# One pool of PSUM banks, exps of one to three banks, plain loads of x, and a new order for a gated mix of two attentions

## The chip, the core and the metric

The kernel runs on one core of a Trainium2 chip. The metric is device time in microseconds, 673.3 before the change (median of two runs, 673.2 and 673.4). A core has five engines with a queue each, worked off in order: TensorE (PE, whose weight loads the profile lists apart as PEld), VectorE (DVE), ScalarE (ACT), GpSimd (POOL) and SyncE (SP), which here only issues DMAs. Engines wait for each other through semaphores. PE writes its results into PSUM, eight banks of 512 fp32 columns on 128 partitions; ACT and DVE read them there and write SBUF.

## The reference

Two attentions over the same x (2048 rows of 512, 32 heads of width 16) are mixed by a gate of each row. A is linear attention with a learned feature map, B is softmax attention:

```python
x = A_x
g = sigmoid((x * gate_w).sum(-1, keepdims=True))

# A: q, k, v = x @ A_wqkv, split into heads
phi = lambda t: concat([softmax(t @ w_phi), softmax(-(t @ w_phi))])   # per head
kv, z = phi(k).T @ v, phi(k).sum(rows)
a = (phi(q) @ kv) / (phi(q) @ z + 1e-6) @ A_wo

# B: q, k, v = x @ B_wqkv, split into heads
p = softmax(q @ k.T * 16 ** -0.5)                                     # 2048 x 2048 per head
b = (p @ v) @ B_wo

return g * a + (1 - g) * b
```

Nearly all of the time goes into B's 32 x 2048 x 2048 exponentials and the matmuls before and behind them.

## The kernel before

**Blocks and tiles.** B's attention is cut into 32 blocks. A block has four heads (one in each quarter of the partitions) and one chunk of 512 queries. Its scores are 64 tiles: for each of the 16 tiles of 128 keys and each of the four heads one matmul of 32 rows (16 of them real) that writes a whole bank with 128 keys by 512 queries (`qk_mm`, line 966). The four heads' matmuls use different rows of PE's array and can run side by side. In all there are 2048 such tiles.

**Two ways to an exponential.** A tile goes one of two ways. On ACT's way one activation (line 1057) reads two neighbouring banks and writes `exp` to the buffer `E`. On DVE's way a `tensor_scalar` (line 1043 for one bank, 1033 for a pair of banks in one instruction) adds a constant and writes the sum as int16, whose bits are a coarse exponential in bf16; POOL then adds fixed steps to the words (`int64_add`, line 1019) for a second and a third, shifted copy, and the three are summed by the matmuls that follow, which evens the error out. A group is four such tiles, with two buffers for its copies. The constant list `DN` says how many tiles of each block go to DVE, 744 in all in 195 groups; the other 1304 are ACT's, in 652 exps.

**Sums over keys.** The weighted sum of the values (and, by a column of ones, the softmax denominator) is made by matmuls of 32 columns each (`pv_mm`, line 1078), four heads side by side on different columns of the array: one such round for a tile of keys from ACT, three for a group from DVE. All rounds of a block add up in one bank, `psO`. When the block is complete, DVE copies the bank out (line 1172), the denominators go through memory by several DMAs on SP (`ld`, `lq`), are inverted (line 1181), spread by two more steps (`lr`, `rb`) and multiplied in (line 1188). The last two blocks are turned on DVE instead (lines 1198 to 1208).

**Banks.** Six banks `S0` to `S5`, one `M` and one `O`. The exps of ACT alternate between `S0, S1` and `S2, S3`, so the scores of an exp are written when the exp two places before has been read. `S4`, `S5` and `M` serve DVE's tiles and all projections; `O` is the sum's.

**Around it.** All projections (`fill`, with `columns` on line 727 or full-width matmuls), A's feature maps (two exps on ACT for each, line 1334), its sums and its quotient, and the output projections (`out_tile`, `out_part`, `out_last`) are put between the work of B's attention wherever a bank is free. For two output tiles, 14 and 15, the part that needs no result of the last blocks is made ahead into `osum` (line 1262) and the rest is added later (line 1232).

**x.** PE needs x transposed. The first 512 rows come by four plain loads (line 651), on SP and ACT, and are transposed on PE against an identity (line 1453), with copies by ACT and DVE (lines 1459 and 1462). The other 1536 rows come by twelve transposing DMAs on SP (line 655).

**The order.** `Plan` holds every operation with what it reads and writes. `TABLE` gives each engine's order as a list of operation numbers, and, in `homes`, the bank of each result; a planner had made it ahead of time, with costs and due times that stand among the constants. `place` follows the lists, makes each operation that takes a bank wait for the one that last read it, and `emit` writes out the instructions with their semaphore waits.

## Time and profile before

| | |
|---|---|
| median of two runs | 673.3 us |
| span of the profiled execution | 675.3 us |
| PE busy | 660.0 us, 8695 instructions |
| ACT busy | 642.5 us, 723 instructions |
| DVE busy | 605.0 us, 965 instructions |
| POOL busy | 404.9 us, 432 instructions |
| mean granted TensorE clock | 0.989 |
| DMA | 30.92 MB |

The page gives the profiled execution's span, from the first to the last instruction, 675.3 us; its own time is not given apart from that. Busy time of PE counts each matmul from its start to the end of its pipeline, and matmuls overlap, so a busy PE is not one at its peak. In a line of a group, the first number behind the bar is the time the engine was busy with the group, the second the mean of one instruction in ns, and then follows the idle time just before them, with what ended it. In a line of the order of time, the first number is the start, the second the length, and a bracket holds the idle time before it.

### The profile page before, as it was taken

What the parts mean: (1) busy time and instruction counts of PE and PEld (TensorE: products, weight loads), DVE (VectorE), ACT (ScalarE), POOL (GpSimd) and SP (SyncE); (2) the same over time, 40 slices, a digit from 0 to 9 for tenths busy, and PEclk for the clock granted to TensorE, in tenths of its full rate; (3) what the DMA queues carried; (4) which work ended last, traced back from release to release, by engine and by line L of the source; (5) the groups of instructions that cost most, each with busy time, mean ns of one, the idle gap of its engine ahead of it and who ended that gap; (6) DMA issues with size and microseconds to landing.
All of it is one profiled execution on the core that took longest, in us unless ns stands there. A gap on an engine that the chain in (4) does not pass through costs nothing.

```text
span 675.3 us, 20326 instructions
## 1 busy us (share of the span) xinstructions
PE 660.0 (98%) x8695; PEld 226.8 (34%) x8695; DVE 605.0 (90%) x965; ACT 642.5 (95%) x723; POOL 404.9 (60%) x432
## 2 busy tenths in 40 slices
PE   8999999999999999989999999999999999999997
PEld 4332333434233333323233233322333232332332
DVE  4698889999998889989989999899999989999994
ACT  5999999999999999989999999999989998899995
POOL 7055466556656445656576776656675567565853
PEclk8999999999999999989999999999999999899999
DMA  7810101001010000000103222141112522034131
GB/s 127 171 26 11 31 14 27 9 7 29 7 27 11 14 16 9 16 16 9 27 26 78 79 49 74 39 110 42 29 42 70 110 51 77 17 84 95 27 95 33
DMA packets 67466, 30.92 MB, mean 46 GB/s; under 512 B 52696, under 2 KB 62296, under 8 KB 67376
## 3 DMA queue, kind: packets, MB, share of 16 engines
q1 hardware_dynamic: 66368, 28.95, 19.3%
q8 instruction: 68, 1.11, 0.8%
q10 hardware_dynamic: 576, 0.52, 0.2%
q0 software_dynamic: 432, 0.15, 0.2%
q14 instruction: 22, 0.18, 0.1%
HBM read 7.87 MB, written 8.88 MB: 25 GB/s over the span
## 4 chain that ended last, share of the span: by engine, by line
PE 63%; ACT 24%; DVE 7%; DMA 3%; SPq 2%; issue 1%; ACTq 0%; DVEq 0%
PE psO L1078 24%; PE psS L966 22%; ACT E_t L1057 22%; PE psS L727 12%; PE psS L1341 2%; DVE Tx_t L1043 2%; ACT EA_t L1334 1%; PE psS L818 1%; DVE Ty_t L1043 1%; DMA xT_t<-in_A_x_dram 1%; PE psS L831 1%; ACT phiK_t L1334 1%; DMA Lq_t<-ld 1%; DVE Wp_t L1043 1%; PE psS L1381 1%
## 5 line engine op out<-in xcount | busy, mean ns | idle before, releaser
L1057 ACT ACTIVATE E_t<-psS 128x1024 bf16<-128x1024 f32 x652 | 612.3, 1079 | 21.6 <-PE psS L966 18.2
L966 PE MATMUL psS<-qz_t,kTB_t 32*128 32x512 bf16 x2048 | 279.8, 386 | 8.6 <-ACT E_t L1057 2.6
L1043 DVE TENSOR_SCALAR Tx_t<-psS 128x512 int16<-128x512 f32 x260 | 170.7, 680 | 11.8 <-PE psS L966 10.8
L966 PEld LDWEIGHTS psS<-qz_t,kTB_t 32*128 32x128 bf16 x2048 | 74.3, 91 | 245.3 <-ACT E_t L1057 98.0
L1078 PE MATMUL psO<-E_t,vaug_t 128*32 128x512 bf16 (+1 forms) x1304 | 107.5, 389 | 0.0
L1019 POOL INT64_ADD vA_t<-vA_t x72 | 73.0, 1017 | 31.4 <-PE psO L1078 24.1
L1043 DVE TENSOR_SCALAR Ty_t<-psS 128x512 int16<-128x512 f32 x114 | 76.3, 683 | 7.9 <-PE psS L966 7.1
L1019 POOL INT64_ADD Ty_t<-Tx_t x29 | 29.7, 1023 | 37.2 <-DVE Tx_t L1043 31.6
L1078 PE MATMUL psO<-vA_t,vaug_t 128*32 128x512 bf16 x520 | 50.8, 384 | 0.0
L1019 POOL INT64_ADD Ty_t<-Ty_t x42 | 43.6, 1038 | 11.2 <-PE psO L1078 11.1
L1043 DVE TENSOR_SCALAR Tz_t<-psS 128x512 int16<-128x512 f32 x66 | 44.4, 683 | 6.1 <-PE psS L966 5.7
L1043 DVE TENSOR_SCALAR oT_t<-psS 128x512 int16<-128x512 f32 x60 | 40.5, 684 | 4.6 <-PE psS L966 4.3
L1078 PE MATMUL psO<-Ty_t,vaug_t 128*32 128x512 bf16 x436 | 44.2, 387 | 0.0
L1078 PEld LDWEIGHTS psO<-E_t,vaug_t 128*32 128x32 bf16 (+1 forms) x1304 | 26.8, 96 | 39.4 <-issue 27.7
L1043 DVE TENSOR_SCALAR vA_t<-psS 128x512 int16<-128x512 f32 x56 | 37.7, 682 | 1.9 <-PE psS L966 1.5
L1043 DVE TENSOR_SCALAR Wp_t<-psS 128x512 int16<-128x512 f32 x52 | 35.0, 684 | 2.6 <-PE psS L966 2.1
L1043 DVE TENSOR_SCALAR WAT_t<-psS 128x512 int16<-128x512 f32 x54 | 36.2, 682 | 1.1 <-PE psS L966 0.4
L727 PE MATMUL psS<-xT_t,WB_t 128*32 128x512 bf16 x480 | 36.8, 393 | 0.0
L727 PE MATMUL psS<-Wp_t,xT_t 128*32 128x512 bf16 x512 | 36.2, 382 | 0.0
L1019 POOL INT64_ADD vA_t<-Tx_t x22 | 21.9, 999 | 19.4 <-DVE Tx_t L1043 14.0
L1019 POOL INT64_ADD oT_t<-oT_t x18 | 17.8, 990 | 23.8 <-PE psO L1078 23.8
L1019 POOL INT64_ADD phiQT_t<-Tx_t x19 | 18.4, 971 | 20.1 <-DVE Tx_t L1043 15.7
(159 smaller groups left out, 876.7 us busy)
## 6 DMA issues: line engine op xcount, KB each, us to landing
dpq<-EA_t SPq DMA_DIRECT2D x16, 256.0 KB, 2.4
...
```

Source lines behind the costliest of these rows:

```text
L727: ins = e.matmul(out[32 * i:32 * i + 32, :], lhsT=lhsT[:, 32 * i:32 * i + 32], rhs=rhs, start=start, stop=stop, tile_position=(0, 32 * i))
L818: mms = [lambda e, ap, i=i, t=t: e.matmul(ap[:, 128 * i:128 * (i + 1)], lhsT=xT[:, t, NQ * c + 128 * i:NQ * c + 128 * (i + 1)], rhs=W_B[:, ...
L831: mms = [lambda e, ap, i=i, t=t: e.matmul(ap[:, 256 * i:256 * (i + 1)], lhsT=xT[:, t, NQ * c + 128 * (2 * hf + i):NQ * c + 128 * (2 * hf + ...
L966: return e.matmul(bank, lhsT=kT_B[32 * i:32 * i + 32, ROW[b // 2] % 2, 128 * kt:128 * (kt + 1)], rhs=qz[32 * i:32 * i + 32, b // 2 % 4, b ...
L1019: op = P.add("pool", P64 + W64 * size, d_prio(g["ts"][0]) - 5.0 + (0.0 if key == "s" else M_LATE), lambda e: e.int64_add(words(dst), words ...
L1043: ops.append(drain(f, mm, "dve", 0.70, d_prio(d), lambda e, ap, q=q: e.tensor_scalar(quarter(tb, q).bitcast(I16), ap, EXPB, 0.0, op0=ALU.a ...
L1057: op = P.add("act", EXP_OVH + 0.4267 * n, 0.0, lambda e: e.activation(Ebuf[:, j // 2 % EPAIRS, 512 * SZ[0] * (j % 2):512 * SZ[0] * (j % 2) ...
L1078: return e.matmul(psO[32 * i:32 * i + w, :], lhsT=vaug[:, kt, o:o + w], rhs=rhs, start=start, stop=stop, tile_position=(0, 32 * i), skip_g ...
L1334: ins = e.activation(dst.rearrange("p (g s c) -> p s g c", s=2, c=64)[:, sgn, :, :], ap.rearrange("p (g c) -> p g c", c=64), ACTF.Exp, sca ...
L1341: mms = [lambda e, ap, n=n, f=f: e.matmul(ap[:, 64 * n:64 * n + 64].rearrange("p (s g j) -> p s g j", s=2, j=4), lhsT=ident[:], rhs=es[n][ ...
L1381: ins = e.matmul(ap[64 * s:64 * s + 64, 68 * gg:68 * gg + 68], lhsT=phiK[:, m, 128 * g + 64 * s:128 * g + 64 * s + 64], rhs=vA[:, m, s, g, ...
```

## The change

One tensor `ps` holds all eight banks, and scores, projections and sums take any of them: every single score tile is now an operation with a bank of its own (`tile_mm`), and each block's sum has its own `Fill` in the pool, so that two blocks' sums can be open at the same time. An exp reads one, two or three banks at equal distance, as the string `sizes` says (620 of two, 17 of three, 5 of one), and writes them side by side into a ring of 24 slots of `E`. `acts` lists the tiles of keys that ACT takes (four heads each, 324 of them, 1296 tiles), `groups` those that DVE takes (188 groups of four heads, 752 tiles) with the buffers of their copies. A sum's round is always the four heads of one tile of keys. Pairs of DVE's tiles in one instruction go from 41 to 71. The planner's constants (costs, priorities, due times) are gone from the kernel; the order of each engine's list, the banks and the pairs are new throughout.

x comes by seven plain loads, five on SP and two on ACT, and all 16 tiles are transposed on PE (line 1453 before, now in a loop over `NT`), 15 of the copies on DVE and one on ACT.

What each block and each projection computes is unchanged.

```diff
+ESLOTS = 24
+XLOADS = (("sp", 0, 1), ("act", 1, 2), ("sp", 2, 3), ("act", 3, 4), ("sp", 4, 8), ("sp", 8, 12), ("sp", 12, 16))
+XACT = (1,)
+WENG = ("sp", "pool", "sp", "sp", "sp", "sp")
...
-    psS = ctx.enter_context(nc.psum_tensor("psS", [128, 3584], F32))
-    psO = ctx.enter_context(nc.psum_tensor("psO", [128, 512], F32))
-    psM = psS[:, 3072:3584]
-    bS = [Bank(f"S{i}", psS[:, 512 * i:512 * (i + 1)], i) for i in range(6)]
-    bO = Bank("O", psO[:])
-    bM = Bank("M", psM, 6)
...
+    ps = ctx.enter_context(nc.psum_tensor("ps", [128, 4096], F32))
+    ps3 = ps[:].rearrange("p (a c) -> p a c", c=512)
+    banks = [Bank(f"S{i}", ps[:, 512 * i:512 * (i + 1)], i) for i in range(8)]
...
-    xs = phiK[:, 0:2, :].rearrange("p a b -> p (a b)").rearrange("p (i c) -> p i c", i=4)
-    for i in range(4):
-        dma("sp" if i % 2 == 0 else "act", -0.01, lambda e, i=i: e.dma_start(
-            xs[:, i, :], A_x[0, 128 * i:128 * (i + 1), :]), [("xs", i)], name=f"xs{i}", issue=0.45, lat=2.65 if i < 2 else 2.9)
-    for c in range(1, QC):
-        for t in range(KT):
-            dma("sp", 0.01 * (4 * c + t), lambda e, c=c, t=t: e.dma_start_transpose(
-                xT[:, t, NQ * c:NQ * (c + 1)], A_x[0, NQ * c:NQ * (c + 1), 128 * t:128 * (t + 1)]),
-                [("xT", t, c)], name=f"x{c}_{t}", issue=1.4, lat=3.9)
+    xs = phiK[:].rearrange("p a b -> p (a b)").rearrange("p (i c) -> p i c", c=D)
+    x_v = A_x[0].rearrange("(i p) c -> p i c", p=128)
+    for n, (eng, lo, hi) in enumerate(XLOADS):
+        dma(eng, lambda e, lo=lo, hi=hi: e.dma_start(xs[:, lo:hi, :], x_v[:, lo:hi, :]), [("xs", i) for i in range(lo, hi)],
+            name=f"xs{n}")
...
+    def tile_mm(b, i, kt, name, after=()):
+        f = Fill()
+        op = P.add("pe", lambda e: e.matmul(f.ap(), lhsT=kT_B[32 * i:32 * i + 32, ROW[b // 2] % 2, 128 * kt:128 * (kt + 1)],
+                                            rhs=qz[32 * i:32 * i + 32, b // 2 % 4, b % 2, :], start=True, stop=True,
+                                            tile_position=(32 * i, 0)),
+                   reads=[kkey(ROW[b // 2], kt), ("q", b // 2 % 4, b % 2)], after=after, name=name)
+        op.acq, op.att, op.shape = f, ("s", b, kt, i), ("row", i)
+        return f, op
...
+    def add_round(quad, parts, reads, name, after=()):
+        b, kt = divmod(quad, 16)
+
+        def fn(e):
+            for i in range(4):
+                ins = pv_mm(e, b, i, kt, parts(i), op.opens, op.closes)
+            return ins
...
-        op = P.add("act", EXP_OVH + 0.4267 * n, 0.0, lambda e: e.activation(
-            Ebuf[:, j // 2 % EPAIRS, 512 * SZ[0] * (j % 2):512 * SZ[0] * (j % 2) + 512 * n], psS[:, 512 * base:512 * (base + n)], ACTF.Exp, scale=ESCALE),
-            reads=[("S", j % 2)], writes=[("E", j % ERING)], name=f"exp{j}")
...
+        def fn(e):
+            where = sorted(f.bank.index for f, _ in slot)
+            step = where[1] - where[0] if n > 1 else 1
+            assert step > 0 and all(y - x == step for x, y in zip(where, where[1:]))
+            return e.activation(Ebuf[:, 512 * k:512 * (k + n)].rearrange("p (a c) -> p a c", c=512), ps3[:, where[0]:where[-1] + 1:step, :],
+                                ACTF.Exp, scale=ESCALE)
...
-            P.add("dve", 0.69, -50, lambda e: e.tensor_copy(Tf[:, par, :], psO[:]), reads=["psO"], writes=[("Tf", par)],
-                  after=[pv], name=f"ev.{b}").kind = "ev"
+            P.add("dve", lambda e: e.tensor_copy(Tf[:, par, :], psum(b)), writes=[("Tf", par)], after=pv, name=f"ev.{b}").fills = (P.sums[b],)
...
-    for i in range(4):
+    xe = []
+    for i in range(NT):
         mms = [lambda e, ap, i=i, t=t: e.transpose(ap.bitcast(BF16)[:, 128 * t:128 * (t + 1)],
                                                    xs[:, i, 128 * t:128 * (t + 1)], ident[:]) for t in range(KT)]
```

The beginning of the new lists of SP and PE, with the numbers written out as operations: SP issues x tile 2, the first keys' weights, x tile 0, x tiles 4 to 7, x tiles 8 to 11, the first values' weights, x tiles 12 to 15. PE transposes x tiles 1, 0, 2 and 3, makes the first queries and keys, transposes tiles 7 and 4, begins the first values, transposes tile 5, ends the first values, and then makes the first three score tiles.

994 lines of the change are left out of this document (374 added, 620 removed), and 519 rows, old and new, of the table TABLE.

## The prediction

> **What bounds the kernel now.** I read the page's busy shares first, then the same by stretches of time, then the groups, then the waits, and last the order of time in four places: start, a full stretch, two holes, the end.
>
> ```profile
> PE 660.0 (98%) x8695; PEld 226.8 (34%) x8695; DVE 605.0 (90%) x965; ACT 642.5 (95%) x723; POOL 404.9 (60%) x432
> ```
>
> ```profile
> 0.00:10.00 10.00, 8.30 (x61) 4.95 (x61) 6.60 (x26) 4.24 (x6) 8.91 (x18) 1.00 0.75 151
> 10.00:20.00 10.00, 8.73 (x78) 3.63 (x78) 1.55 (x3) 6.94 (x8) 4.51 (x9) 0.66 0.71 99
> 20.00:665.00 645.00, 636.00 (x8443) 215.44 (x8446) 592.70 (x929) 627.24 (x707) 390.28 (x405) 0.99 0.19 43
> 665.00:676.00 11.00, 6.95 (x122) 2.79 (x114) 4.14 (x7) 4.04 (x5) 1.17 (x2) 0.93 0.15 49
> ```
>
> The columns are the stretch, its length, then PE, PEld, DVE, ACT and POOL busy, the granted clock, and DMA. ACT stands still for 32.8 us of the 675.3: 5.8 before 10 us, 3.1 up to 20, 17.8 in the 645 us of the middle, 6.3 at the end (665 to 675.3). PE is busy almost throughout, but that row counts a matmul's pipeline, so the waits must say whether PE waits or makes others wait.
>
> ```profile
> PEld psS L966 <- ACT E_t L1057: 98.0, 239, 0.8
> PEld psO L1078 <- issue: 82.6, 330, 0.4
> ACT E_t L1057 <- PE psS L966: 18.2, 41, 1.5
> ```
>
> PE's weight load waits 239 times for an exp to give a bank back, 0.41 us each; where it waits for nothing the pause is 0.25 (82.6/330). So about 0.16 x 239 = 38 us are real waits of PE for ACT, against 18.2 us in 41 waits of ACT for PE. ACT bounds the middle, with PE a close second, and DVE (592.7 of 645) third. What ACT needs at least:
>
> ```profile
> L1057 ACT ACTIVATE E_t<-psS 128x1024 bf16<-128x1024 f32 x652 | 612.3, 1079 | 21.6 <-PE psS L966 18.2 <-PE psO L1078 2.3
> L1334 ACT ACTIVATE phiK_t<-psS 128x512 bf16<-128x512 f32 x32 | 18.3, 660 | 0.0
> 308.62 22.23 ACT L1057 ACTIVATE E_t<-psS 128x1024 bf16<-128x1024 f32 x24 [0.23 <-PE psS L966]
> ```
>
> One exp of two banks lasts 1.079 us, but 24 in a row take 22.23, which is (22.23 - 1.08)/23 = 0.92 from one to the next. All 652 at that pace are 600 us.
>
> **The change part by part.** Counts are from both kernels' written-out orders, each number matched to its operation by the order in which the builder makes them.
>
> *Exps.* 652 of two banks become 620 of two, 17 of three, 5 of one (the string of sizes); 1304 tiles become 1296. A three-bank or one-bank exp is not in the trace. The nearest rows are 1024 columns (1079) and 512 columns (660): a bank more or less is 0.42 us. So 620 x 0.92 + 17 x 1.34 + 5 x 0.50 = 595.7, **-4.1 us** on the engine that bounds. More is excluded, since no row shows a bank under 0.42. Bounds: -3.6 if a bank costs half of a two-bank exp (0.46), 0 if a read of three banks, which need not adjoin, takes 0.24 longer than that (4.1/17).
>
> *DVE's tiles.* 744 become 752, and pairs in one instruction 41 become 71.
>
> ```profile
> L1043 DVE TENSOR_SCALAR Ty_t<-psS 128x512 int16<-128x512 f32 x114 | 76.3, 683 | 7.9 <-PE psS L966 7.1
> L1033 DVE TENSOR_SCALAR Ty_t<-psS 128x1024 int16<-128x1024 f32 x7 | 8.5, 1218 | 0.0
> L1019 POOL INT64_ADD vA_t<-vA_t x72 | 73.0, 1017 | 31.4 <-PE psO L1078 24.1 <-DVE vA_t L1043 7.1
> ```
>
> Before 662 x 0.683 + 41 x 1.22 = 502 us, after 610 x 0.683 + 71 x 1.22 = 503: nothing. POOL's adds go from 390 to 376 at 1.02 us; POOL is 60% busy and the rest of its time hides any change; without that cover it would be -14 us.
>
> *PE in the middle.* Sums of a block come in whole rounds of four matmuls: 343 + 585 = 928 rounds before (ACT's tiles and three for each of 195 groups, some only half filled), 324 + 3 x 188 = 888 after. Scores come in bursts between them: 583 before, 643 after.
>
> ```profile
> 661.25 0.61 PE L727 MATMUL psS<-WoB_t,oT_t 128*32 128x512 bf16 x8
> 661.79 0.39 PE L966 MATMUL psS<-qz_t,kTB_t 32*128 32x512 bf16 x2
> 662.11 0.40 PE L727 MATMUL psS<-WoB_t,oT_t 128*32 128x512 bf16 x4
> 662.33 0.60 PE L727 MATMUL psS<-WoA_t,phiK_t 128*32 128x512 bf16 x8
> ```
>
> A round starts 0.22 after the last (662.11 to 662.33). Two rounds and the way into a burst take 0.54, so the way in costs 0.11; burst to round takes 0.32, so the way out costs 0.10. A burst thus costs 0.21 beside its matmuls. Rounds: -40 x 0.22 = -8.8. Bursts: +60 x 0.21 = +12.6. Matmuls that queue on the same rows of the array inside a burst: 724 become 715, -1.9. Together about **+2** of PE work. More matters where it falls. I went through both orders and added up PE's work between the last scores of one exp and of the next. Before, 219 of 581 such stretches are above ACT's 0.92, by 75 us in all, and the trace made 17.8 us of idle ACT of that. After, 276 of 600 are above it, by 93. In the same proportion ACT idles 22.1: **+4.3 us**. Bounds: 0 (PE's 38 us of waiting takes it), +18 (all of the growth is paid).
>
> Of the Trainium skill, "TensorEngine Tiling (Array Packing)", section Key Properties, speaks against this change: a change of tiling mode drains TensorE. The 0.11 and 0.10 agree with it in kind; by that rule alone each of the 60 bursts more would put 0.21 on the path, and the sum below would be 8 us higher.
>
> *One pool of banks.* Before, an exp's two banks are fixed and its scores wait for the exp two places earlier. In the new table, of the 581 exps that take a bank over from ACT, 559 still take it from two places earlier, 18 from three, 4 from the one before. So the pool deepens nothing for ACT. It does let a block's sum start in another bank while the last one is still being read, and the trace has one place where that hurts, and one where DVE waits for a reciprocal's way through memory:
>
> ```profile
> 570.00:580.00 10.00, 9.48 (x121) 3.11 (x113) 8.54 (x12) 7.19 (x9) 6.92 (x8) 0.83 0.06 16
> 576.42 1.89 PE L1078 MATMUL psO<-E_t,vaug_t 128*32 128x512 bf16 x14
> 577.50 1.94 ACT L1057 ACTIVATE E_t<-psS 128x1024 bf16<-128x1024 f32 x2 [2.34 <-PE psO L1078]
> 290.00:300.00 10.00, 8.49 (x78) 2.59 (x82) 7.87 (x12) 6.82 (x8) 3.67 (x4) 0.83 0.00 0
> 292.40 1.40 DVE L1188 TENSOR_TENSOR oT_t<-Tf_t,Rb_t 128x512 bf16<-128x512 f32 x1 [1.15 <-DMA Rb_t<-lr]
> ```
>
> These two stretches hold 2.8 + 3.2 = 6.0 us of idle ACT. They are accidents of this one order, so a new order does not inherit them: **-6.0**. Bounds: -6.0, and 0 if it has as many of its own (between reciprocal and product it leaves 13 to 20 DVE instructions, against 14 to 26).
>
> *Start.* x chunks 1 to 3 now come by three plain loads and go through 48 more transposes on PE and 12 more copies on DVE, in place of twelve transposing DMAs.
>
> ```profile
> 0.73 0.87 SPq L651 DMA_DIRECT2D phiK_t<-in_A_x_dram  x2
> 2.67 16.54 SPq L655 DMA_TRANSPOSE xT_t<-in_A_x_dram  x12
> 4.57 1.22 PE L1453 MATMUL psS<-ident_t,phiK_t 128*128 128x128 bf16 x12
> 4.82 0.42 DVE L1462 COPY xT_t<-psO 128x512 bf16<-128x512 bf16 x1 [0.69 <-PE psO L1453]
> 7.85 0.40 PE L966 MATMUL psS<-qz_t,kTB_t 32*128 32x512 bf16 x4
> 8.28 3.77 ACT L1057 ACTIVATE E_t<-psS 128x1024 bf16<-128x1024 f32 x4 [1.08 <-PE psS L966]
> 10.00:12.00 2.00, 0.73 (x10) 0.36 (x10) 0.00 (x0) 2.00 (x3) 2.00 (x6) 1.00 0.70 110
> 12.00:19.00 7.00, 7.00 (x57) 2.62 (x56) 1.39 (x2) 4.15 (x5) 1.97 (x4) 0.51 0.74 96
> WvA_t<-in_A_wqkv_dram SPq DMA_DIRECT2D x1, 512.0 KB, 4.3
> ```
>
> SP's queue loses 16.5 us of issues. PE gains 48 x 0.10 = 4.9 us and DVE 12 x 0.42 = 5.0, both where PE had a hole (10 to 12 us) and DVE 8.4 us free. What can be won is ACT's 3.1 us between 10 and 20, when x came late and the clock stood at 0.51. What can be lost: in the new PE order two transposes of chunk 1 and the first values' projection stand ahead of the first scores, and its weights are sixth on SP, behind two of the 512 KB loads. Such a load lands 4.3 us after its issue; two issues take 0.87, so the weights' turn comes near 0.7 + 5 x 0.44 = 2.9 us, and landing 4.3 to 8.6 later is 7.2 to 11.5, against first scores at 7.85 and a first exp at 8.28. So the first exp is 0 to 3.3 later (the projection's own 0.4 would lie on top). I take half of that, 1.6, and the whole gain: **-1.5**; bounds -3.1 and +3.3.
>
> *End.* After the last sum's turn DVE now has two partial outputs and two outputs; before, the first of these partials was done at 663:
>
> ```profile
> 662.56 0.75 DVE L1262 TENSOR_SCALAR xT_t<-psS,gT_t 128x512 f32<-128x512 f32 x1 [0.76 <-PE psS L727]
> 670.34 0.71 DVE L1262 TENSOR_SCALAR xT_t<-psS,gT_t 128x512 f32<-128x512 f32 x1
> 671.14 1.41 DVE L1232 SCALAR_TENSOR_TENSOR WB_t<-psS,gT_t,xT_t 128x512 bf16<-128x512 f32 x2
> ```
>
> One more at 0.71: **+0.7**. Blocks 30 and 31 are now halved between ACT and DVE (32 tiles of 64 each; 32 and 16 were DVE's); I count that at nothing, with up to 2 us won of the 6.3.
>
> *Sum.* 675.3 - 4.1 + 4.3 - 6.0 - 1.5 + 0.7 = 668.7. The timed runs (673.2 to 673.4) lie 2.0 below the profiled span, so **666.7, say 667 us**. With its bounds on the middle the case runs from 658 to 681.
>
> **The rivals.** *The holes close.* ACT's 17.8 idle us in the middle, and the 12 us by which its 612.3 busy us exceed 652 x 0.92, are the price of waiting at all. If the new order feeds ACT steadily, half of these 30 us go instead of 6.0 less 4.3: 667 - 13 = 654. For it: each score tile now has a bank, and a wait, of its own, and the bursts are more even (396 of three). Against it: the distance of two exps is as before, and more stretches are over 0.92.
>
> *PE becomes the bound.* The 60 bursts more and their unevenness are paid in full, 18 in place of 4.3, the two holes come back elsewhere (+6), and the start loses 1.6 instead of winning: 667 + 13.7 + 6.0 + 3.1 = 690. It decides from the point where PE's work between two exps is above 0.92 so often that its 38 us of waits no longer take it up. For it: 276 against 219 such stretches. Against it: total PE work grows by less than 1% of 660.
>
> *It does not do what it says.* The pool is mostly used as the fixed pairs were (559 of 581), tiles and work move by 1%. Then only -4.1 and the start count: 668, which is inside the forecast.
>
> **How the numbers follow.** Forecast 0.35, does not do what it says 0.10 (the same time, so 0.45 for the two), holes close 0.32, PE the bound 0.23. Fewer than 2% from no change is 659.8 to 686.8; about that much a measurement of this kernel can tell. Faster: nearly all of the second case and the low edge of the first, 0.33. Slower: most of the third, 0.19. Within: 0.48. The range goes from 651 (the second case less its start) to 691 (the third). The likeliest case's own range is 658 to 681.
>
> **What would show it.** Exps: the two-bank group at 620 or so and the pace still 0.92. PE: scores' waits for ACT well below 98 us and ACT's wait for scores above 18.2 if bursts cost what I say; the reverse if the holes close. Start: ACT's idle time between 10 and 20 us gone, the first exp near 9 to 10 us. Block changes: no idle ACT of over 2 us put down to the sums. The forecast is wrong if ACT's idle time from 20 us to the last 10 is under 10 us or above 35.

## The result, and the profile after

The changed kernel takes **696.9 us** (median of two runs, 696.4 and 697.4) against 673.3: a ratio of 1.036, with an interval of 1.031 to 1.042. It is slower, and outside the forecast's range (651 to 691). The profiled execution has a span of 694.6 us and was timed at 696.4, so a timed run lies 1.8 above its span; the forecast had set it 2.0 below. One thing is needed to read the times: executions of one and the same kernel differ by some 2% with the TensorE clock that they were granted, so each ratio below is made against runs of the kernel before on the same chip, with disturbed ones left out.

The busy shares and the stretches of the changed kernel, cut as the prediction cut them (stretch, length, PE, PEld, DVE, ACT, POOL busy, clock, DMA):

```profile
PE 673.4 (97%) x8759; PEld 231.6 (33%) x8759; DVE 627.4 (90%) x955; ACT 645.6 (93%) x713; POOL 408.2 (59%) x418
```

```profile
0.00:10.00 10.00, 6.71 (x37) 3.67 (x38) 4.36 (x22) 2.58 (x4) 8.46 (x17) 0.86 0.82 229
10.00:20.00 10.00, 9.50 (x103) 5.54 (x101) 8.35 (x21) 6.59 (x6) 0.00 (x0) 0.97 0.76 154
20.00:684.30 664.30, 650.76 (x8516) 219.94 (x8518) 609.91 (x906) 635.12 (x702) 397.06 (x399) 0.98 0.17 40
684.30:695.00 10.70, 6.45 (x116) 2.47 (x108) 4.81 (x8) 1.27 (x2) 2.64 (x3) 0.92 0.15 51
```

ACT now stands still for 7.4 us up to 10 (5.8 before), 3.4 up to 20 (3.1), 29.2 in the middle (17.8) and 9.0 at the end (6.3). Two waits, and the groups of exps by size with one run of exps in the order of time:

```profile
PEld ps L892 <- ACT E_t L975: 117.9, 303, 0.8
ACT E_t L975 <- PE ps L892: 29.2, 45, 3.9
```

```profile
L975 ACT ACTIVATE E_t<-ps 128x1024 bf16<-128x1024 f32 x620 | 588.2, 1035 | 28.3 <-PE ps L892 24.5 <-PE ps L903 0.8
L975 ACT ACTIVATE E_t<-ps 128x1536 bf16<-128x1536 f32 x17 | 24.7, 1459 | 5.0 <-PE ps L892 4.8
L975 ACT ACTIVATE E_t<-ps 128x512 bf16<-128x512 f32 x5 | 3.0, 606 | 0.0
```

```profile
353.04 18.53 ACT L975 ACTIVATE E_t<-ps 128x1024 bf16<-128x1024 f32 x20
```

A third bank costs 1459 - 1035 = 424 ns, and the pace of two-bank exps in a row is (18.53 - 1.03)/19 = 0.92, both as forecast. Yet ACT is busy with exps for 615.9 us, 20 more than the 595.7 of that pace; before it was 612.3, 12 more than 600. An exp that does not follow the last one closely costs its whole 1.03 in place of 0.92, so idle time alone does not show all that ACT loses. I therefore use one more number. **ACT's loss against its own pace** in a stretch is the stretch's length, less 0.92 for each exp that ends in it (0.42 more or less for each bank beyond or below two), less ACT's other instructions at their own length:

| us | 0-60 | 60-350 | 350-450 | 450-600 | 600-end | sum |
|---|---|---|---|---|---|---|
| before | 9.5 | 4.9 | -1.1 | 7.1 | 8.6 | 29.0 |
| after | 13.9 | 7.9 | 12.1 | 7.4 | 14.1 | 55.4 |
| more | 4.4 | 3.0 | 13.2 | 0.3 | 5.5 | 26.4 |

(Other instructions can overlap with exps, which is why a loss can be below zero.) The 26.4 more, less the 4.1 of the exps, less 3.0 by which ACT's other instructions got shorter (46.5 to 43.5), are the 19.3 by which the span grew. Half of the growth lies between 350 and 450 us, most of the rest at the start and the end.

**The stop at 370.** First the stretch in both kernels, before and then after:

```profile
350.00:450.00 100.00, 98.11 (x1238) 32.34 (x1230) 94.93 (x156) 99.62 (x114) 66.13 (x68) 1.00 0.27 69
```

```profile
350.00:450.00 100.00, 94.04 (x1141) 31.30 (x1129) 87.55 (x131) 89.08 (x100) 56.52 (x54) 0.90 0.24 59
370.10:373.40 3.30, 0.36 (x7) 0.06 (x3) 1.36 (x3) 1.47 (x2) 2.41 (x3) 0.86 0.57 155
373.40:386.10 12.70, 12.67 (x120) 3.71 (x121) 7.18 (x11) 7.73 (x9) 2.12 (x3) 0.50 0.25 52
```

PE stands for 3 us, and then, though busy, has a clock of 0.50 for 12.7. What it stood for, in the order of time of SP, then of PE and ACT, of the changed kernel, and SP's wait:

```profile
344.33 0.44 SPq L1247 DMA_DIRECT2D dpq<-EA_t  x1
360.60 5.09 SPq L1253 DMA_TRANSPOSE phiQT_t<-dpq  x4
366.38 1.72 SPq L1253 DMA_TRANSPOSE WAT_t<-dpq  x1
371.05 0.43 SPq L1247 DMA_DIRECT2D dpq<-EA_t  x1
...
373.43 1.05 PE L709 MATMUL ps<-Wp_t,xT_t 128*32 128x512 bf16 x8 [2.97 <-DMA dpq<-EA_t]
...
375.08 2.11 ACT L975 ACTIVATE E_t<-ps 128x1024 bf16<-128x1024 f32 x2 [3.52 <-PE ps L892]
```

```profile
SPq L1253 <- PE ps L709: 15.2, 1, 15.2
```

The projection at 373.43 (row 6 of A's feature map, `P0.6`) must not begin until the store of an earlier `EA` buffer (`pw4`) has left it. That buffer was ready at 359.7, but its store is issued at 371.05, because it stands on SP behind transposing loads (`Tq0`) of 1.25 us each, and the first of these waits 15.2 us for the sum's round `pm.87`, whose data were ready at 354.5 and which PE's list brings only at 360.2. (The view names L709, the matmuls right behind that round; that it is the round, the run `a_pm87` shows.) So one round, late on PE, stops SP, which stops PE ten microseconds later.

The data do not ask for this wait. The load writes `phiQT`, and the last round that reads it runs at 352.27; `pm.87` reads the group's other buffer, in `Tx`:

```profile
352.27 0.39 PE L903 MATMUL ps<-phiQT_t,vaug_t 128*32 128x512 bf16 x4
360.16 0.40 PE L903 MATMUL ps<-Tx_t,vaug_t 128*32 128x512 bf16 x4
```

The load waits all the same, because the kernel makes it depend on every operation of every group that used the buffer (`op.deps + wp_ops + users["pt"]`, line 1357 of the changed kernel). No run takes this dependency away, so what that would win is not shown.

**Start and end.** Rows of PE and ACT of the changed kernel, in the order of time:

```profile
6.44 0.84 PE L1293 MATMUL ps<-ident_t,phiK_t 128*128 128x128 bf16 x12 [2.00 <-DMA phiK_t<-in_A_x_dram]
11.38 0.61 PE L795 MATMUL ps<-WB_t,xT_t 128*128 128x128 bf16 x8
12.59 0.39 PE L892 MATMUL ps<-qz_t,kTB_t 32*128 32x512 bf16 x3
13.08 2.50 ACT L975 ACTIVATE E_t<-ps 128x1536 bf16<-128x1536 f32 x2 [3.93 <-PE ps L892]
...
683.08 1.02 ACT L975 ACTIVATE E_t<-ps 128x1024 bf16<-128x1024 f32 x1 [2.24 <-PE ps L892]
687.45 0.72 DVE L1041 STREAM_TRANSPOSE Tf_t<-ps 128x512 f32<-128x512 f32 x1 [3.43 <-PE ps L903]
690.16 1.27 ACT L1116 ACTIVATE WB_t<-ps,gT_t 128x512 bf16<-128x512 f32 x2 [6.06 <-PE ps L709]
```

x tile 0 is third on SP, and PE stands 2.00 us for it, until 6.44 (the same transposes began at 4.57 before). The first values come at 11.38, right behind other work, without a pause for their weights. The first exp comes at 13.08 (8.28 before). At the end, DVE is busy to 683.7:

```profile
655.00:683.70 28.70, 27.59 (x338) 8.58 (x330) 28.30 (x39) 25.17 (x27) 25.57 (x25) 1.00 0.20 43
```

DVE has 28.30 of 28.7 us, ACT three and a half to spare. DVE's last tiles go through POOL and PE before the last sum can be turned at 687.45, 3.4 us after the last exp is done.

### The profile page after: what moved, and what is told of

Same layout as the page of the kernel before. It is cut to its first block, busy times and chain, and to the rows that moved or that the text cites. A ratio compares the mean times of both kernels' runs of the same rounds, so it can differ in the third digit from the quotient of the medians.

```text
span 694.6 us, 20402 instructions
## 1 busy us (share of the span) xinstructions
PE 673.4 (97%) x8759; PEld 231.6 (33%) x8759; DVE 627.4 (90%) x955; ACT 645.6 (93%) x713; POOL 408.2 (59%) x418
## 4 chain that ended last, share of the span: by engine, by line
PE 73%; DVE 14%; SPq 4%; ACT 3%; DMA 3%; issue 2%; POOL 1%; DVEq 0%
PE ps L892 27%; PE ps L903 26%; PE ps L709 13%; SPq L1253 3%; ACT E_t L975 3%; PE ps L1182 2%; DVE vA_t L938 2%; DVE vA_t L933 1%; PE ps L795 1%; DVE oT_t L1032 1%; PE ps L808 1%; DMA WAT_t<-dpq 1%; DVE Tz_t L938 1%; DVE oT_t L938 1%; PE ps L1278 1%
## 5 line engine op out<-in xcount | busy, mean ns | idle before, releaser
L975 ACT ACTIVATE E_t<-ps 128x1024 bf16<-128x1024 f32 (+1 forms) x642 | 613.8, 1043 | 33.2 <-PE ps L892 29.2
L892 PE MATMUL ps<-qz_t,kTB_t 32*128 32x512 bf16 x2048 | 287.9, 389 | 7.1 <-DVE vA_t L938 1.4
L892 PEld LDWEIGHTS ps<-qz_t,kTB_t 32*128 32x128 bf16 x2048 | 74.5, 91 | 242.4 <-ACT E_t L975 117.9
L903 PE MATMUL ps<-E_t,vaug_t 128*32 128x512 bf16 (+1 forms) x1296 | 122.7, 388 | 0.1
L938 DVE TENSOR_SCALAR oT_t<-ps 128x512 int16<-128x512 f32 x128 | 84.1, 683 | 5.1 <-PE ps L892 4.6
L919 POOL INT64_ADD Tx_t<-Tx_t x45 | 47.2, 1050 | 43.1 <-PE ps L903 43.0
L938 DVE TENSOR_SCALAR vA_t<-ps 128x512 int16<-128x512 f32 x104 | 68.3, 681 | 2.7 <-PE ps L892 2.2
L919 POOL INT64_ADD vA_t<-vA_t x49 | 51.2, 1048 | 29.3 <-PE ps L903 16.5
L938 DVE TENSOR_SCALAR phiQT_t<-ps 128x512 int16<-128x512 f32 x60 | 40.6, 686 | 5.9 <-PE ps L892 5.4
L709 PE MATMUL ps<-Wp_t,xT_t 128*32 128x512 bf16 x512 | 42.5, 390 | 3.1 <-DMA dpq<-EA_t 3.0
L903 PE MATMUL ps<-vA_t,vaug_t 128*32 128x512 bf16 x464 | 45.1, 389 | 0.4 <-POOL vA_t L919 0.4
L709 PE MATMUL ps<-xT_t,WB_t 128*32 128x512 bf16 x480 | 37.5, 383 | 0.6 <-DVE Ty_t L933 0.6
L933 DVE TENSOR_SCALAR vA_t<-ps 128x1024 int16<-128x1024 f32 x24 | 29.2, 1221 | 1.6 <-PE ps L892 1.5
```

Of the source, the lines that this page charges most:

```text
L709: ins = e.matmul(out[32 * i:32 * i + 32, :], lhsT=lhsT[:, 32 * i:32 * i + 32], rhs=rhs, start=start, stop=stop, tile_position=(0, 32 * i))
L892: op = P.add("pe", lambda e: e.matmul(f.ap(), lhsT=kT_B[32 * i:32 * i + 32, ROW[b // 2] % 2, 128 * kt:128 * (kt + 1)], rhs=qz[32 * i:32 * ...
L903: return e.matmul(P.sums[b].ap()[32 * i:32 * i + w, :], lhsT=vaug[:, kt, o:o + w], rhs=rhs, start=start, stop=stop, tile_position=(0, 32 * ...
L919: op = P.add("pool", lambda e: e.int64_add(quarters(dst).bitcast(I64), quarters(src).bitcast(I64), step * 0x0001000100010001), reads=[(src ...
L933: return e.tensor_scalar(quarters(t)[:, a[0]:a[1] + 1:a[1] - a[0], :].bitcast(I16), ps3[:, c[0]:c[1] + 1:c[1] - c[0], :], EXPB, 0.0, op0=A ...
L938: d = P.add("dve", lambda e, i=i, f=f: e.tensor_scalar(quarters(t)[:, group.places.index(i), :].bitcast(I16), f.ap(), EXPB, 0.0, op0=ALU.a ...
```

## The experiments

In the diffs a list of an engine is shown by the names of its operations, with a minus where one was taken out and a plus where it was put. `X` and `Xe` are the transposes of an x tile and their copy; `Q`, `K` and `V` the projections of B; `qk` the scores of an exp; `ps`, `pt` and `pm` the three rounds of a group, `D` its tiles on DVE; `pw` and `Tq` the store and the transposing loads of A's query features; `Z` and `N` A's products for the denominator and the numerator; `wob` the load of B's output weights.

### Both kernels once more

**a_again** and **b_again**: the changed kernel and the kernel before.

```diff
(nothing changed)
```

> The changed kernel itself once more, as the base for the runs beside it: near 697 us, ratio 1.036 to 1.04. If the stop before P0.6 belongs to the order and not to one execution, this profile has it again: P0.6 over 3 us late behind pw4, 0.50 of the clock behind it, ACT's loss of 11 to 13 us between 350 and 450.

The changed kernel ran 693.9 us, 1.038 (1.034 to 1.041) times the kernel before on that chip, with losses of 13.9, 7.8, 10.2, 6.5 and 14.1. Its profile has the stop again, 2.87 us, and 13.7 us at half clock from 371.9 on: it belongs to the order, not to one execution. The loss of the stretch from 350 to 450, though, is 10.2 here and 12.1 in the first profile: that much differs from one execution to the next.

> The kernel before once more, for its profile alone. If the holes near 294 and 576 us belong to its order, they are there again, with ACT's loss of about 5 us in 250 to 300 and 6 in 550 to 600; if they come from one execution's clock, this profile has the clock at 1.00 there and a loss under 2 and 4.

One time of the kernel before, 680.4 us, with losses of 16.0, 3.0, -1.1, 5.2 and 9.1. In the stretches of the two holes on which the forecast's -6.0 rested the clock is now 1.00, and the loss is smaller: from 250 to 300 it is 1.8 (5.0 in the first profile), from 550 to 600 it is 3.1 (6.4). ACT's wait behind a new block's sum is still there in the second, 1.48 us in place of 2.34. This execution lost at the start instead; its rows in the stretches:

```profile
0.00:20.00 20.00, 17.75 (x145) 8.99 (x149) 8.22 (x29) 12.51 (x15) 13.39 (x26) 0.82 0.65 126
20.00:60.00 40.00, 38.97 (x324) 11.57 (x316) 28.05 (x43) 33.63 (x36) 10.41 (x11) 0.75 0.35 74
12.70:40.00 27.30, 27.30 (x189) 8.15 (x187) 11.89 (x18) 19.55 (x20) 1.77 (x3) 0.50 0.62 127
```

For 27.3 us PE is never idle, and its clock is 0.50 throughout.

### The stop between 350 and 450

**q_pw.** Stores first on SP:

```diff
 SP: ... pw3
+pw4, pw5
 Tq0.0 ... Tq0.4
-pw5
 Tq0.5
-pw4
 Tq0.6 ...
```

> The changed kernel, with one edit in SP's list alone: the two stores of the feature maps of row tiles 4 and 5 to memory (pw4, pw5) are issued ahead of the eight transposing loads Tq0, instead of between them. In the changed kernel's trace the projection P0.6 starts 3.36 us late, 0.04 us after pw4 landed, and the granted clock is 0.50 from 372.5 to 386.1; ACT's loss against its own pace is 7.7 us in 350 to 400. Theory 'a queue on SP stops PE': both stores land some 5 us before PE wants them, the stop and the half clock behind it go, ACT loses about 1 us in that stretch, and the time falls by 6 to 8 us, to about 690 (ratio to before 1.025). Rival 'PE has too much work between the exps': PE was behind anyway, the 3.4 us are made good only in part, and the time falls by 0 to 3 us, to 694 to 697.

693.9 us, 1.035 (1.029 to 1.041); loss between 350 and 450 of 10.2, which is also what the unchanged `a_again` has: the 6 to 8 us of the theory did not come. The wait at 373 is gone, but its neighbours on the same late queue come next, in the order of time of DVE and PE of this kernel:

```profile
371.46 0.35 DVE L1050 RECIPROCAL rd_t<-Lq_t 128x32 f32<-128x32 f32 x1 [1.51 <-issue]
...
372.42 0.39 PE L917 MATMUL ps<-qz_t,kTB_t 32*128 32x512 bf16 x2 [1.02 <-DVE WAT_t L963]
```

**a_fill.** Idle matmuls in place of the wait (fifteen rounds of four on zeros, so that PE does not stand):

```diff
 PE: ... 
+15 x idle round
 P0.6.0 ...
```

> The changed kernel with 15 rounds of matmuls on zeros (four of 512 columns each, 0.22 us a round, into the bank that the projection P0.6 takes next) ahead of P0.6. They fill the 3.36 us in which PE waits for pw4 there; the wait itself stays. Theory 'the half clock behind the stop costs as much as the stop': PE does not pause, the clock stays at 1.00 from 370 to 390, ACT's loss in 350 to 400 falls from 7.7 us to about 4.5, and the time falls by about 3 us. Rival 'only the wait counts': the loss stays at 7 or more and the time within 1 us. The other rival, 'the clock falls whether PE waits or not': 0.50 appears there all the same.

702.3 us, 1.047 (1.043 to 1.051), slower still; loss 12.1. PE's order of time and two stretches of this kernel:

```profile
369.80 3.42 PE L1392 MATMUL ps<-xT_t,zero_t 128*32 128x512 bf16 x60
388.09 0.32 PE L1304 MATMUL ps<-kzbd_t,phiQT_t 128*128 128x64 bf16 x4 [3.05 <-DVE vA_t L964]
```

```profile
373.40:388.10 14.70, 11.64 (x169) 4.40 (x161) 10.03 (x16) 12.15 (x14) 7.21 (x7) 1.00 0.26 62
389.40:395.00 5.60, 5.60 (x48) 1.39 (x48) 3.82 (x6) 3.94 (x4) 1.04 (x1) 0.50 0.02 3
```

With PE kept busy the clock stays at 1.00 through the same wait and up to 388; there PE stands for 3 us on the next late step, and only then the clock falls. This is `N2`, A's product of queries and sums, which by the lists needs the store `ow0` of an earlier result on the same queue (the bracket names DVE; in the profile of `a_nostop`, below, the same matmul's wait of 0.87 us is put down to that store, `dpo<-kv_t`). The clock follows PE's standing here, and the idle rounds themselves, without a store that comes sooner, win nothing. That the kernel became 8 us slower was in neither theory; the profile has the rest of the loss behind the stretch, 12.9 from 450 to 600 (6.5 in `a_again`), with 13.7 us at half clock from 579 on.

**a_nostop.** The whole chain of steps behind the late queue put later or earlier:

```diff
 SP:  pw4 after Tq0.3; wob after Tq1.7
 PE:  Z0 after pt.94; Z1 after qk812; N5 after qk815; Z3, N12, N13 after ps.149
 DVE: rd15 after D94.3; T2.15 after D97.0; na0, nb0, na1, nb1 later
```

> The changed kernel with the three places mended where PE stands for a DMA. SP: pw4 directly after Tq0.3, the load of the output weights of B after Tq1.7 instead of among the Tq1. PE: Z0, Z1 and Z3 (which need the last of Tq0, Tq1, Tq3) 1 to 3 us later. DVE: the reciprocal of blocks 14 and 15, T2.15 and the steps behind Z0 and Z1 a few places later, so that DVE does not stand for the same queue. Theory 'a queue on SP stops PE, DVE and then the clock': ACT's loss between 350 and 450 us falls from 12.1 to 3 or less, half clock between 350 and 600 from 23.9 us to under 7, and the time falls by 8 to 11 us, to 685 to 688. Rival 'PE is too slow there anyway': the loss stays above 7 and the time falls by less than 5.

695.0 us, 1.039 (1.035 to 1.042); loss 8.2. The long stop is gone, PE's waits between 366 and 400 are 0.68, 0.87 and 0.57, and ACT still idles thirteen times, for 0.25 to 1.34 us, between 378 and 450. In loss and time this is what the rival said, above 7 and less than 5 us won.

**a_pm87.** The late round brought forward, and the two stores with it:

```diff
 PE: ...
+pm.87
 K3.1.0 ...
-pm.87
 SP: Tq0.3
+pw4, pw5, Tq0.4
```

> The changed kernel with the reason for the backlog on SP taken away: Tq0 overwrites a buffer that DVE's group 87 still uses, and waits on SP for the last sum of that group (pm.87), which PE makes 5.7 us after it could, while SP stands for 15.2 us and then issues 18 of the next 20 us. PE's list has pm.87 some 5 us earlier, and SP issues pw4, pw5 and Tq0.4 directly after Tq0.3. Theory 'the backlog starts there': Tq0.0 is issued near 355.5 instead of 360.6, no DMA is late for PE between 360 and 395, ACT's loss in 350 to 450 falls from 12 to 5 or less and the time by 6 to 8 us. Rival 'the stop moves on to the next DMA in the queue, as when pw4 alone was moved': the loss stays at 9 or more and the time within 3 us.

690.4 us, 1.031 (1.026 to 1.036), 3.5 us below the changed kernel in the same comparison (693.9). The transposing loads now start at 356.0 in place of 360.6, right behind the round, and the loss is 7.4. Of the edits in this stretch it is the one whose time fell, and the stores alone (`q_pw`) had won nothing; but 8.5 of the 13.2 us remain. PE still stands 0.83 us at 383 and 0.66 us at 430, with 3.4 and 6.8 us at half clock behind them. Theory (the backlog starts at this round) and rival (the stop moves on to the next step) each hold in part.

### Is PE the bound?

**a_thin** and **b_thin.** The third round of each group, four matmuls of 512 columns, cut to one matmul of 8. This leaves the third shifted copy's share out of the sums:

```diff
-rhs[:, :], out=[0:32, 0:512]
+rhs[:, 0:8], out=[0:32, 0:8]        # third round of a group, unless it opens or closes a sum
```

> The changed kernel with less work for PE: of the three rounds of matmuls that sum each of DVE's groups, the third is cut to one matmul of 8 columns (unless it opens or closes a block's sum), so the third shifted copy is left out of the sums. At 0.22 us a round this takes about 32 us of PE's 673 away, spread evenly over the middle. Theory 'single holes, the start and the end make the difference': PE's spare time was not what was short; the time falls by 5 to 12 us, to 685 to 692, and stays 15 us or more above the kernel before with the same cut. Rival 'PE is the bound of the new order': the time falls by 20 us or more, to 677 or below, and the distance to the kernel before with the same cut shrinks to less than 8 us.

697.7 us, 1.038 (1.030 to 1.047): no gain, though some 32 us of PE's work is gone. Part of what it may have won is hidden: three of its four executions have mean clocks of 0.968 to 0.971 (0.979 and 0.980 in the changed kernel). The fourth, the profiled one, has 0.984 and a span of 688.1, with a loss of 4.8 from 60 to 350 (7.9) and still 11.7 and 14.1 in the stop's stretch and at the end.

> The kernel before with the same cut of PE's work (the third round of each of DVE's groups is one matmul of 8 columns): some 33 us less for PE. ACT bounds the middle by the reading of the profile, and PE waits 38 us for it, so the time falls by 2 to 10 us, to 663 to 671. If PE bounds this kernel as well, it falls by 15 us or more.

The same cut in the kernel before makes it **slower**, in all four executions: 689.1 us, 1.028 (1.023 to 1.033), where 663 to 671 was expected. One of its stretches:

```profile
11.10:48.70 37.60, 37.60 (x262) 10.67 (x260) 16.98 (x26) 26.60 (x27) 6.09 (x9) 0.50 0.52 98
```

37.6 us at half clock from 11 us on, and 66.6 in the whole execution (16.7 in the first profile of the kernel before). So the two cut kernels are only 8.6 us apart, where the theory wanted 15 and the rival less than 8; that distance says more of the clock than of PE's work. From 60 to 350, where the clock matters little, the loss of `b_thin` is 1.5 (2.2 to 4.9 in four executions that are uncut there) and that of `a_thin` 4.8 (7.8 and 7.9): the cut lowers it in both, and 3.3 stay between the two. So PE's amount of work has some weight, but 32 us less of it bring a few us and not the 20 of a kernel that it bounds.

### The holes of the kernel before

**b_holes.** The steps whose waits made the two holes, put past DVE's work that stood behind them:

```diff
 DVE:
+T2.11
 ... D1.13.13.3
-T2.11
+T2.25
 ... D1.27.15.3
+ev.26
 D1.27.14.3
 PE:
+pv551.27
 dq27.13.3.0
```

> The kernel before with four instructions moved: on DVE the product T2.11 four places later (it waited 1.15 us for the reciprocals from memory), T2.25 four places earlier and with it the copy ev.26 (which frees the one bank of sums) one tile earlier; on PE the first sum of block 27 ahead of three score tiles. Theory 'the two holes are accidents of the order and cost 5.0 and 6.4 us of ACT in their stretches': the loss between 250 and 300 us falls from 5.0 to about 1, between 550 and 600 from 6.4 to 3 or less, and the time falls by 5 to 8 us, to 0.99 of the kernel before. Rival 'the time lost there is needed elsewhere (DVE and PE are behind anyway)': within 2 us of the kernel before.

671.2 us against 670.5, a ratio of 1.002 (1.000 to 1.004): mending both holes wins nothing. The first was mostly that one execution's: its loss is 2.3 here, 1.8 in `b_again`, and 2.3 again in `b_warm` (below), whose order is unmended there. The second is not. ACT's wait behind a new block's sum comes in the other executions of that order too, here in `b_again` and `b_warm`:

```profile
ACT E_t L1057 <- PE psO L1078: 1.5, 1, 1.5
ACT E_t L1065 <- PE psO L1086: 2.2, 1, 2.2
```

The four moved steps take this wait away, and yet the loss from 550 to 600 is 7.0, at a clock of 1.00, where 3 or less was expected; without the moved steps it is anything from 3.1 (`b_again`) to 7.0 (`b_warm`). What the wait cost, other steps took up, as the rival said.

### The start

**s_both.** First scores before the second chunk's transposes, with x tile 0 and the first weights at the head of SP:

```diff
 SP:
+xs0, xs2, wbk0, wbv0
 xs4 ...
 PE: ... K0.0
+qk0, qk1, qk2
 K0.01
-X7, X4, V0.0, X5, V0.0, qk0, qk1, qk2
+V0.0, qk4, qk3, X7, X4, X5, X6, X8, X9
```

> The changed kernel with another start: SP issues x tiles 0 and 2 and the first weights of keys and values ahead of the three 512 KB loads; PE makes the first three score tiles as soon as the first queries and keys are there, and the transposes of x tiles 7, 4 and 5 and the first values after them (banks and DVE's list to match). Theory 'the first loads come late because they share the way with the large ones, and PE's order puts their transposes in front': x tile 0 lands near 3.4 instead of 6.39, the first exp starts near 8.5 to 9 instead of 13.08, and the time falls by 3 to 4.5 us, to 692 to 694. Rival 'the start is made good later': x tiles 4 to 15 and the first values come as late as before, the exps stop there instead, and the time falls by less than 1.5 us.

698.0 us, 1.042 (1.037 to 1.046); loss up to 60 of 13.9, the same. ACT's order of time shows why:

```profile
9.16 1.45 ACT L1000 ACTIVATE E_t<-ps 128x1536 bf16<-128x1536 f32 x1 [1.12 <-PE ps L917]
12.33 1.02 ACT L1000 ACTIVATE E_t<-ps 128x1024 bf16<-128x1024 f32 x1 [1.72 <-PE ps L917]
16.14 1.45 ACT L1000 ACTIVATE E_t<-ps 128x1536 bf16<-128x1536 f32 x1 [2.79 <-PE ps L917]
```

The first exp comes 3.9 us sooner, the third no sooner than before (16.14; 15.89 in the changed kernel).

**a_xdma.** The loads of x chunks 1 to 3 by twelve transposing DMAs, as before the change, with the first loads first on SP:

```diff
-XLOADS = (..., ("sp", 4, 8), ("sp", 8, 12), ("sp", 12, 16))
+XLOADS = (...)                      # chunk 0 alone; 12 dma_start_transpose for the rest
-PE: X4 ... X15      DVE: Xe4 ... Xe15
 PE: V0.2, V0.3 later
```

> The changed kernel with one part of the change undone: x chunks 1 to 3 come by twelve transposing DMAs on SP again, so 48 transposes on PE and 12 copies on DVE are gone; the first loads stand first on SP, and the first values' projections of chunks 2 and 3 stand behind their loads. The changed kernel loses 13.9 us of ACT up to 60 us, the kernel before 9.5 with the clock at half for 6.8 us. Theory 'the transposes and their copies stand ahead of the first exps in PE's and DVE's lists': the loss up to 60 us falls to 9 or less and the time by 4 to 5 us against the changed kernel beside it (693.9). Rival 'the order of the first scores does it, not x': the loss stays at 12 or more, the time within 2 us.

697.7 us, 1.041 (1.036 to 1.045); loss up to 60 of 13.0, 0.9 less than in the changed kernel. This does not show what the plain loads cost: behind a pause of PE of 0.98 us this execution has 10.2 us at half clock (11.1 to 21.4), and at the 0.4 us for each that is worked out at the end these would be about 4 of the 13, by estimate. Taken off, the loss is 9, the theory's figure; left on, it is the rival's.

**a_start2.** First loads as in `s_both`, and the transposes and scores of the first chunk interleaved by hand, one or two transposes between the scores of the next six exps:

```diff
 PE: qk0..2, K0.01, qk4, qk3, qk5..7,
+X7, X4, qk8..10, X5, X6, ...
```

> The changed kernel with its loads as they are (x by plain loads, only the small first ones ahead of the large) but another order of PE's and DVE's first operations: the scores of the first three exps come before the transposes of x tiles 4 to 15, which follow one or two at a time between the scores of the next six, each in bank 3 or 7. Taking the loads back left the loss up to 60 us at 13.0 (13.9 in the changed kernel). Theory 'the order of the first operations makes the loss': it falls to 10 or less, the first exps run without a pause from 9 us on, and the time falls by 3 to 4 us against the changed kernel (693.9 on this sort of chip). Rival 'the work itself, 48 transposes and 12 copies, has to be done in that time anyway': the loss stays at 12 or more.

697.9 us, 1.041 (1.034 to 1.048). Loss up to 20 falls to 7.9, but 8.8 come between 20 and 60, in sum 16.7. ACT's rows (stretches, then the order of time):

```profile
0.00:20.00 20.00, 15.22 (x145) 7.89 (x145) 13.98 (x42) 12.24 (x12) 10.79 (x21) 1.00 0.82 191
20.00:60.00 40.00, 37.40 (x461) 13.97 (x457) 33.59 (x53) 32.50 (x36) 21.12 (x24) 1.00 0.07 19
```

```profile
20.98 3.28 ACT L1000 ACTIVATE E_t<-ps 128x1536 bf16<-128x1536 f32 x3 [2.45 <-PE ps L917]
28.87 1.94 ACT L1000 ACTIVATE E_t<-ps 128x1024 bf16<-128x1024 f32 x2 [2.50 <-PE ps L917]
33.43 16.39 ACT L1000 ACTIVATE E_t<-ps 128x1024 bf16<-128x1024 f32 x18 [2.63 <-PE ps L928]
```

What ACT wins early it pays by 33 us. Part of these three pauses are waits of 1.3 us each that my own placing of the values' projections made. Of the three changed starts none lessened the loss as it was measured, and in `a_xdma` the half clock stands in the way of saying why.

### The end, and all together

**a_all.** The last group of four tiles (187) from DVE to ACT, with the edits of `a_nostop` and the first loads of `s_both`:

```diff
+acts += [504]
-groups
+groups[:-1]
+sizes += "22"
```

> All of the former run and two more edits of the changed kernel: SP issues x tiles 0 and 2 and the first weights ahead of the 512 KB loads (its list alone, no other change at the start), and the last of DVE's groups (four tiles of block 31) is given to ACT as two more exps, with the block's sums ahead of the partial outputs in PE's list. Theory 'DVE is the last to finish, by three and more tiles, because it has half of the last two blocks': DVE's last tile ends near 681 less what the former edits win, the last sum is closed about 2.5 us earlier against the end, and with 1 us at the start the time falls 3 to 4 us below the former run, to 681 to 685. Rival 'the end is bound by PE's list': no more than 1 us below the former run.

695.9 us, 1.039 (1.036 to 1.042), where 681 to 685 was expected. From 650 us on, the loss is 2.7 less than in `a_nostop` (13.4 to 10.7), as expected, and ACT's last wait falls from 6.06 to 5.43 us. But from 350 to 450 the loss is 12.0 again (8.2 in `a_nostop`), with 17.1 us at half clock there (10.2): what the end won, the middle lost.

**a_best.** `a_pm87`, the first loads, `wob` after `Tq1.7`, and group 187 on ACT:

```diff
+a_pm87's edits, xs0 xs2 wbk0 wbv0 first, wob after Tq1.7, group 187
```

> The former run with the first loads reordered on SP, the load of B's output weights behind Tq1, and the last group of DVE's tiles given to ACT. If each of the parts (the first loads 2 us, the backlog 6 to 8, the end 2.5) adds up, 12 us below the changed kernel, near 685; if the losses only move, within 4 us of it.

688.9 us, 1.028 (1.025 to 1.031), 5 us below the changed kernel beside it, with losses of 11.2, 7.2, 4.0, 11.4 and 12.8. With `a_best2`, which follows, it is the best of the new order.

**a_best2.** With more of A's late products put later:

```diff
+a_best, and Z3, N12, N13 after ps.149
```

> The run with pm.87 earlier, the first loads reordered and the last group given to ACT (688.9), and Z3 with N12 and N13 some 1.5 us later in PE's list: there PE stood 1.83 us for the last Tq3, with 13.7 us at half clock behind it and a loss of 8.6 us in 550 to 600. Theory 'stop and half clock belong together': no half clock there, a loss of 5 or less, 684 to 686. Rival 'the place is slow anyway': 688 to 690.

689.8 us, 1.027 (1.022 to 1.032), losses 11.2, 7.9, 6.5, 10.2 and 12.4: the rival's figure. Of the half clock behind that place 10.2 us are left. Its six executions run from 684.0, at a mean clock of 1.00, to 694.2 at 0.982.

**a_best3.** With the old loads of x:

```diff
+a_best2, and x by transposing DMAs as in a_xdma
```

> The former run with x chunks 1 to 3 by transposing DMAs. If the terms add up (start 4 to 5 us below the former run): 680 to 682, a third of the distance to the kernel before left, which would be the list of PE itself; if not, above 684.

692.7 us, 1.033 (1.029 to 1.036), loss up to 60 of 13.9: no gain. Here too the start has half clock, 6.8 us from 13.6 on, where `a_best2` has none; by the same estimate that is 2.7 us, the whole of the difference to its 11.2.

**a_best4.** With the other start:

```diff
+a_start2, a_pm87's edits, wob after Tq1.7, group 187
```

> The former run with pm.87 earlier, the load of B's output weights behind Tq1 and the last group given to ACT (together 688.9 with the other start). If the start's 2 us come on top: 686 to 688, and 682 to 683 in executions at full clock; if not, 689 or more.

691.4 us, 1.029 (1.025 to 1.034), losses 16.7, 7.9, 2.8, 10.2 and 11.5: the middle's gain is kept, the start's loss too.

### The kernel before, with PE kept busy at 10 us

PE has two short pauses there, 0.53 us for ACT and 0.41 for x (rows of the kernel before, run once more, on PE; the columns as in each order of time):

```profile
10.25 0.39 PE L966 MATMUL psS<-qz_t,kTB_t 32*128 32x512 bf16 x2 [0.53 <-ACT E_t L1057]
11.05 0.38 PE L818 MATMUL psS<-WB_t,xT_t 128*128 128x128 bf16 x4 [0.41 <-DMA xT_t<-in_A_x_dram]
```

**b_warm.** Rounds of four matmuls on zeros fill them, in a bank that is free then:

```diff
+_pe[at qk3:at qk3]       = [-3] * 4      # -3: an idle round
+_pe[at V0.1.0:at V0.1.0] = [-3] * 3
```

> The kernel before with seven rounds of matmuls on zeros in two places near 10 us where PE stands 0.9 and 0.8 us, four ahead of the fourth scores and three ahead of the first values of chunk 1. Theory 'half clock follows a standstill of PE': the clock is 1.00 from 10 us on, no execution has the 6.8 to 27 us at half clock that the kernel before has there in some, and the time is within 1 us of its undisturbed executions, 669 to 671. Rival 'it is the load, not the standstill': half clock appears there all the same in some.

**667.8 us**, 0.995 (0.992 to 0.997) times the kernel before, whose median on that chip is 672.1. This is less than the 2% that would count as clearly faster, but the interval is clear of 1, and it beats both kernels. Its stretches:

```profile
0.00:20.00 20.00, 18.51 (x190) 9.21 (x191) 8.49 (x30) 13.39 (x16) 13.43 (x26) 1.00 0.68 126
20.00:60.00 40.00, 38.96 (x406) 12.45 (x404) 34.91 (x55) 40.00 (x45) 13.72 (x15) 1.00 0.35 74
```

The clock is 1.00 in both stretches, where it was 0.82 and 0.75 in the repeated run above. Twelve executions lie between 667.4 and 671.0 with mean clocks of 0.997 to 1.000; the seventeen of the kernel before beside them go from 669 to 685, with clocks from 0.973. This agrees with the theory but does not prove it alone: `b_holes`, with no idle rounds, also had twelve executions of 0.995 or more. And eight of the twelve lie 1 to 1.6 us below the fastest of the kernel before, 669.0 at a clock of 1.00; where that comes from is not shown.

## Why the prediction was wrong, point by point

The forecast was 667, the likeliest of its cases; 696.9 lies beyond its range. In changes of ACT's loss its sum was -1.5 at the start, -1.7 in the middle (4.3 less 6.0) and +0.7 at the end; measured were +4.4, +16.5 and +5.5. The exps' -4.1 stands in both. The range of 658 to 681 that the prediction gives the case is not that of its middle: the bounds of the middle alone, 0 to 18 and -6.0 to 0, give 662 to 686.

**Exps, DVE's tiles, POOL: right.** The third bank is 424 ns against the 0.42 assumed, the pace of 0.92 is unchanged, and the read of three banks at a distance shows no extra. DVE's tiles take 489 us (491 before). POOL's adds take 397 (393) though they are 14 fewer. What neither the forecast nor the idle time counted is that fewer exps follow closely.

**PE's work between two exps: right in size.** Leaving the stop aside, the loss grows by 3.0 from 60 to 350 and by 0.3 from 450 to 600; against the kernel before in other executions (2.2 to 4.9 and 5.2 to 8.0) the changed kernel has 3 to 6 more in the first and about none in the second. The forecast's 4.3, with bounds of 0 and 18, holds. That the bursts make it is not shown: with PE's work cut in both kernels (`a_thin`, `b_thin`) 3.3 stay between them.

**The pool does not deepen ACT's distance: not tried by itself.** Nothing in the runs speaks against it; 303 waits of PE for ACT (239 before) say that scores still wait for the exp.

**The holes, -6.0: the step that failed.** I wrote that the two holes "are accidents of this one order, so a new order does not inherit them", with 0 as the bound if it has as many of its own. Two things were wrong. The holes were not worth 6.0: the first was mostly an accident of one *execution*, with a loss of 5.0 there and 1.8 to 2.3 in three others, and the second, which comes again, won nothing when it was mended (`b_holes`: 7.0, where the first profile has 6.4). And the new order has holes of its own that are larger, by 13.2 us in one stretch: a bound of 0 was far too tight. I had looked at one path in both orders, from reciprocal to product, and counted the instructions in between; the queue that decides, SP's, I did not follow. It could have been read from the new kernel: `pw4` stands behind six loads, and the first of these depends on a round that PE's list brings late. What shows it is `a_pm87`, with that round earlier: 3.5 us of time and 2.8 to 4.7 of loss went. The rest of the 13.2 stays open. A step that the change moves must be checked against each queue that it passes, and this one was not.

**The start, -1.5: failed, sign and size.** The first exp comes at 13.08, 4.8 us later, where I had 0 to 3.3. I made the weights of the first values the step that decides and took the middle of 7.2 to 11.5. The projection did begin at 11.38, the far end, but PE came to it from other work and did not stand for the weights. What made it late, against the kernel before: x tile 0, 1.9 us (6.44 for 4.57), on which the forecast had no term; 1.4 more for the first queries and keys (7.40 to 10.71, where the kernel before had 5.93 to 7.85); and the transposes and first values ahead of the first scores, 10.71 to 12.59, which are 1.9 where I left 0.4 on top. I also counted ACT's 3.1 us between 10 and 20 as won: they are still 3.4. That the first exp as such is the cause, however, `s_both` does not support: with it at 9.16 the loss is the same. Nor do the other two runs on the start name the cause: without the transposes and copies of x (`a_xdma`) half clock fills the gain, and with the scores ahead of them (`a_start2`) the loss comes later. Which part of the work up to 30 us sets the loss isn't settled.

**The end, +0.7: failed.** I counted the halving of the last two blocks "at nothing", with a gain as the other bound. DVE's 64 tiles in place of 48 keep it busy for 28.30 of the 28.7 us to 683.7, the last exp waits 2.24 us for its scores, and the last sum waits for POOL's adds behind DVE's last tiles. `a_all` and `a_best` give four of these tiles back and win 2.7 and 2.9 us there.

**From span to time.** 2.0 was taken off, where 1.8 goes on: 4 us of error by itself, from setting one execution's span against others' times.

**The rivals.** "PE becomes the bound", 690, came nearest in time, and by the wrong way: its 13.7 of bursts and its +6 of holes elsewhere were forecast together, and of these only the second happened (13.2 in place of 6); the loss at the start, its third term, happened too. "The holes close" has nothing for it. The rule on draining at a change of tiling mode would have put 12.6 us on the path in place of 4.3; the middle outside the stop, at +3 to +6, lies nearer to the proportion that I used, but no run sets the two against each other.

**The signs.** I asked for scores' waits for ACT "well below 98 us" if bursts cost what I say: they rose to 117.9, while ACT's wait for scores rose as well, from 18.2 to 29.2. Both grow when PE's work comes unevenly; the pair was no test. And the mark "above 35" for idle ACT in the middle stood too high: 29.2 was enough to be wrong by 30 us, because the start, the end and the lost overlap are not in it. The sign for the sums came true, 0.8 us of idle ACT put down to them (2.3 before), and the time did not follow it.

**What stays open.** The fastest execution of the new order (of `a_best2`) takes 684.0 us with the clock at 1.00, where `b_warm` and the kernel before, so run, have 667 to 669. In their profiled executions, which are 20.1 apart, the losses of `a_best2` are above those of `b_warm` (6.8, 2.2, -1.9, 8.0 and 7.9) by 4.4 up to 60, 5.7 from 60 to 350, 8.4 from 350 to 450, 2.2 from 450 to 600 and 4.5 at the end. The causes of the first two are not settled, and 8.4 of the stop's stretch is left even with the round moved.
